# Gate and skip sums all on VectorE, and the token-count product four chunks behind its one-hot rows

## The chip, the cores and the metric

The kernel runs on one core of a Trainium2 chip. The metric is the device time of one execution in microseconds (us); lower is better. The engines named below are TensorE (PE in the profile; PEld is its weight load, which runs beside the products), VectorE (DVE), ScalarE (ACT), GpSimd (POOL) and SyncE (SP), which issues most of the DMAs.

## The reference

Three layers follow one another: attention with head mixing, a dense two-matrix layer, and a mixture of eight experts with a skip. The change lies where the second layer hands over to the third.

```python
def _moe_ref(x, w_in, w_out):                  # 1792 tokens, 768 -> 2048 -> 768
    h = x @ w_in
    g = np.where(h > 0.0, h, np.exp(np.minimum(h, 0.0)) - 1.0)
    return g @ w_out                           # "the second dense product"

def _moe2_ref(x, w_skip, w_gate, w1, w2):      # E = 8 experts, 768 -> 1024 -> 768
    do_compute = x @ w_skip > 0                # the skip sum
    out = x.copy()
    xc = x[do_compute]
    logits = xc @ w_gate                       # the eight gate sums
    e_idx = np.argmax(logits, axis=1)
    ...
    for e in range(E):
        mask = e_idx == e
        h = np.maximum(xc[mask] @ w1[e], 0.0)
        y[mask] = gate_w[mask, None] * (h @ w2[e])
    out[do_compute] = xc + y
    return out
```

## The kernel before, in words

All products are made in a split form: each fp32 operand is a rounded part and a rest, and three products (high by high, low by high, high by low) are summed. The scheduler of the kernel's framework sets the order of instructions on each engine, except in attention, whose order is written by hand. Each engine works through its own list in order, and so does each DMA queue.

**The second dense product** (from 650 us to about 916 us of the span) goes over 14 tiles of 128 tokens, numbered 0 to 13. Each tile sums over 16 chunks of the hidden dimension, n = 0 to 15; a chunk is six products (L859), three for each half of the 768 output columns, so a tile is 96 products. ScalarE and VectorE split the hidden values of the next tile meanwhile (`gh`, L735 and L736, four per tile). When chunk 15 of tile i is done, ScalarE copies the two halves from the accumulators `o` to a row tile `x` (L890), which SyncE writes to DRAM (`x2d` and `out`). The last nine chunks of tile 12 alternate with the first nine of tile 13. In tile 13 the halves have 512 and 256 columns, and from chunk 10 on the wide half is finished first.

**Scoring.** `score` (L740) multiplies the row tile by nine rows of weights (eight gates, one skip, broadcast in `wrow`) and sums each product along the row. Three of the nine products (e = 0, 3, 6) are made on GpSimd (`prod`, L748) and summed on ScalarE (L749); six are multiplied and summed by one VectorE instruction each (`junk`, L755).

**Routing.** `route(i - 1)` is called in tile i behind chunk 11 (15 in tile 1). VectorE finds the best expert (MAX and MAX_INDEX) and makes a one-hot row `oh` per token. TensorE counts tokens per expert in two products into `pp`: ones by `seen` (all tokens before this tile, L778) and an upper triangle by `oh` (L779). VectorE adds `oh` to `seen`, reads the token's place from `pp` (`ps`, `sl`, `slot`, `si`), and GpSimd scatters the token's number and gate weight to its place in `slots` in DRAM (L797).

**The tail.** The first tokens of expert 0 don't go through DRAM for the last two tiles. After `route(11)`, SyncE reads the first 128 places from `slots` into `pre` (L877) and GpSimd gathers their rows from `x2d` into `xp` (L864). For tile 13 the scores are made on TensorE: `score_turned` transposes the row tile (`tx`, L844), ScalarE copies it, and `logits` multiplies it by the gate weights (`lg`, L835). `place_old` (L825) multiplies `xp` by the identity and the rows of tile 12 by a placement matrix `hot` into `pt` (L830, L831); the rows of tile 13 follow (L905). ScalarE and VectorE split `pt` into `xt`, and the first expert's product `ph` (L1056) begins.

Weights of the experts (`w1t`, L1015) are loaded by SyncE as buffers of the second layer come free; the first is split (`whi` on ScalarE, `wlo` on VectorE) during tile 2. After the tail, eight experts follow, to 1101 us.

Of the kernel before, what the change touches and what calls it, by code (L numbers as in the profile page):

```python
# [8 lines left out]
FP32 = mybir.dt.float32  # L9
# [3 lines left out]
ACTF = mybir.ActivationFunctionType  # L13
ALU = mybir.AluOpType
# [5 lines left out]
NT, DM, DFF = B * S, H * D, 2048  # L20
NK = DM // 128
NF = DFF // 128
NTILE = NT // 128
E, F2 = 8, 1024
# [22 lines left out]
OLD = NTILE - 2  # L47
CUT, SPLIT, SKEW = 512, 10, 9
AT_SCORE, AT_ROUTE, AT_FIRST = 8, 18, 11


R0, RC, LOOK = 3, 2, 2
# [382 lines left out]
def mixtures(tc, order, xT, w_in, w_out, w_skip, w_gate, w1, w2, ident, gT, wf, wg, x2d, slots, out):  # L435
# [4 lines left out]
    nc = tc.nc  # L440
    with ExitStack() as top:
# [6 lines left out]
        ones = keep.tile([128, 128], FP32, name="ones")  # L448
        nc.vector.memset(ones, 1.0)
        upper = keep.tile([128, 128], FP32, name="upper")  # L450
# [6 lines left out]
        def behind(op):  # L457
            return tc.issue_after(op.ins) if op else ExitStack()
# [10 lines left out]
        with ExitStack() as ctx:  # L469
# [151 lines left out]
            w = wi[0] = ring_a.tile([128, 2, DM], FP32R, tag="w", name="w")  # L621
# [72 lines left out]
            last = elu(7)  # L694
# [3 lines left out]
            for s in range(2 * B, len(groups)):  # L698
                products(s)
                last = elu(s)  # L700
# [5 lines left out]
        with ExitStack() as ctx:  # L706
# [5 lines left out]
            st_p = pool("st", 3, ctx)  # L712
# [9 lines left out]
            seen = keep.tile([128, E], FP32, name="seen")  # L722
# [17 lines left out]
            def score(x2, cols=slice(0, DM)):  # L740

                lg = st_p.tile([128, E + 1], FP32, tag="lg", name="lg")
                x2, n, part = x2[:, cols], cols.stop - cols.start, 0
                for e in range(E + 1):
                    w = wrow[:, e, cols]
                    if e % 3 == 0:
                        p = st_p.tile([128, DM], FP32, tag="prod", name="prod", bufs=2)
                        nc.gpsimd.tensor_tensor(out=p[:, :n], in0=x2, in1=w, op=ALU.mult)  # L748
                        nc.scalar.activation(out=p[:, :n], in_=p[:, :n], func=ACTF.Copy, accum_out=lg[:, e:e + 1])  # L749
                    else:  # L750
                        if part == 0:
                            t = st_p.tile([128, DM], FP32, tag="junk", name="junk", bufs=1)
                        o = part * n
                        part = (part + 1) % (DM // n)
                        nc.vector.scalar_tensor_tensor(out=t[:, o:o + n], in0=x2, scalar=1.0, in1=w, op0=ALU.mult,  # L755
                                                       op1=ALU.mult, accum_out=lg[:, e:e + 1])
                return lg

            def route(i, lg):
                mx = st_p.tile([128, 8], FP32, tag="mx", name="mx")  # L760
                nc.vector.max(out=mx, in_=lg[:, :E])
                ix = st_p.tile([128, 8], U32, tag="ix", name="ix")
                nc.vector.max_index(out=ix, in_max=mx, in_values=lg[:, :E])
                nmx = st_p.tile([128, 1], FP32, tag="nmx", name="nmx")
                nc.vector.tensor_scalar(out=nmx, in0=mx[:, 0:1], scalar1=-1.0, scalar2=None, op0=ALU.mult)
                ex = st_p.tile([128, E], FP32, tag="ex", name="ex")
                sm = st_p.tile([128, 1], FP32, tag="sm", name="sm")
                nc.scalar.activation(out=ex, in_=lg[:, :E], func=ACTF.Exp, bias=nmx, accum_out=sm)
                nc.vector.tensor_scalar(out=sm, in0=sm, scalar1=1e-9, scalar2=None, op0=ALU.add)
                nc.vector.reciprocal(out=pairs[:, i, 1:2].bitcast(FP32), in_=sm)  # L770
                ef = st_p.tile([128, 1], FP32, tag="ef", name="ef")
                nc.vector.tensor_copy(out=ef, in_=ix[:, 0:1])
                do = st_p.tile([128, 1], FP32, tag="do", name="do")
                nc.vector.tensor_scalar(out=do, in0=lg[:, E:E + 1], scalar1=0.0, scalar2=None, op0=ALU.is_gt)
                oh = st_p.tile([128, E], FP32, tag="oh", name="oh")
                nc.vector.tensor_scalar(out=oh, in0=iota8, scalar1=ef, scalar2=do, op0=ALU.is_equal, op1=ALU.mult)
                pp = ps_r.tile([128, 512], FP32, tag="r", name="pp")
                nc.tensor.matmul(out=pp[:, :E], lhsT=ones, rhs=seen, start=True, stop=False)  # L778
                nc.tensor.matmul(out=pp[:, :E], lhsT=upper, rhs=oh, start=False, stop=True)  # L779
                nc.vector.tensor_tensor(out=seen, in0=seen, in1=oh, op=ALU.add)  # L780
                ps = st_p.tile([128, E], FP32, tag="ps", name="ps")
                sl = st_p.tile([128, 1], FP32, tag="sl", name="sl")
                nc.vector.scalar_tensor_tensor(out=ps, in0=pp[:, :E], scalar=1.0, in1=oh, op0=ALU.mult, op1=ALU.mult,
                                               accum_out=sl)
                big = st_p.tile([128, 1], FP32, tag="big", name="big")
                nc.vector.tensor_scalar(out=big, in0=do, scalar1=-2.0 * E * CAP, scalar2=2.0 * E * CAP, op0=ALU.mult,
                                        op1=ALU.add)
                place = None
                if i >= OLD:
                    place = wg_p.tile([128, 128], FP32, tag=f"hot{i}", name="hot")  # L790
                    nc.vector.tensor_scalar(out=place, in0=iota128, scalar1=sl, scalar2=do, op0=ALU.is_equal,
                                            op1=ALU.mult)
                slot = st_p.tile([128, 1], FP32, tag="slot", name="slot")
                nc.vector.tensor_tensor(out=slot, in0=sl, in1=big, op=ALU.add)
                si = st_p.tile([128, 1], I32, tag="si", name="si")
                nc.vector.tensor_copy(out=si, in_=slot)
                nc.gpsimd.indirect_dma_start(out=slots, out_offset=bass.IndirectOffsetOnAxis(ap=si[:, 0:1], axis=0),  # L797
                                             in_=pairs[:, i, :], in_offset=None, bounds_check=E * CAP - 1,
                                             oob_is_err=False)
                return place  # L800
# [10 lines left out]
            rows = {}  # L811
# [11 lines left out]
            lg = ps_r.tile([128, 512], FP32, tag="r", name="lg")  # L823
# [24 lines left out]
            for i, n, fc, cs in work:  # L848
                last = i == LAST
# [7 lines left out]
                for a, z in THREE:  # L857
                    for c in cs:
                        mm = nc.tensor.matmul(out=po[c][:, :cols[c].stop - cols[c].start],  # L859
                                              lhsT=gs[i][fc // GC][:, a, fc % GC, :], rhs=wo[fc][:, z, cols[c]],  # L860
# [9 lines left out]
                    logits(turned)  # L870
                if last and n == AT_SCORE:
                    scored = score(rows[i - 1])
                if i and n == (15 if i == 1 else AT_ROUTE if last else 11):
                    hot = old_hot = route(i - 1, scored if last else score(rows[i - 1]))
                    if i == OLD:
                        pre = wg_p.tile([128, 2], I32, name="pre")
                        nc.sync.dma_start(out=pre, in_=slots[0:128, :])  # L877
                        xp = wg_p.tile([128, DM], FP32, name="xp")
                        iota128 = wg_p.tile([128, 128], FP32, name="iota128")
                        nc.gpsimd.iota(iota128, pattern=[[1, 128]], base=0, channel_multiplier=0,  # L880
                                       allow_small_or_imprecise_dtypes=True)
                if fc == NF - 1:
                    if 0 in cs:
                        x2 = rows[i] = x2_p.tile([128, DM], FP32, tag="x2", name="x2")
                    for c in cs:
                        to, at = x2[:, cols[c]], po[c][:, :cols[c].stop - cols[c].start]
                        if last and c == 0:
                            nc.vector.tensor_copy(out=to, in_=at)
                        else:
                            nc.scalar.copy(out=to, in_=at)  # L890
                        if last and c == 1:
                            turned, freed = score_turned(x2, c)
                            place_old(range(2))
                            logits(turned)
                            place_old(range(2, 5))
                    if 1 in cs:
                        nc.sync.dma_start(out=x2d[i * 128:(i + 1) * 128, :], in_=x2)
                        if not last:
                            nc.sync.dma_start(out=out[i * 128:(i + 1) * 128, :], in_=x2)
            hot = route(NTILE - 1, lg)  # L900
            place_old(range(5, NK))
            xt0 = [gh_p.tile([128, 2, GC, 128], FP32R, tag="gh", name=f"xt0{c}") for c in range(2)]
            for c in range(2):
                for k in range(3):
                    nc.tensor.matmul(out=pt[c][:, k, :], lhsT=x2[:, (c * 3 + k) * 128:(c * 3 + k + 1) * 128], rhs=hot,  # L905
                                     start=False, stop=(k == 2))
# [410 lines left out]
```

## Time and profile before

| | us |
|---|---|
| median of 3 runs | 1108.67 (1106.9 to 1115.65) |
| profiled execution | 1108.77 |
| its span, first to last instruction | 1107.0 |
| PE busy in the span | 1024.1 (93%) |
| VectorE busy | 802.3 (72%) |
| ScalarE busy | 566.7 (51%) |
| GpSimd busy | 390.7 (35%) |

The span lies 1.77 us under the profiled execution's own time. Rows of the timeline give the start, the length, the engine, the line and operation, what is written from what is read, how many instructions are merged in the row, and in brackets how long the engine idled before and what ended the wait.

### The profile page before, as it was taken

How to read it: one execution, taken by the hardware profiler on the slowest of the kernel's cores; microseconds unless marked ns; L12 is line 12 of the kernel's file. 1: busy time of each engine (PE TensorE's matmuls, PEld its weight loads, DVE VectorE, ACT ScalarE, POOL GpSimd, SP SyncE). 2: the span in 40 equal slices, each digit the busy share in tenths (PEclk: the TensorE clock that was granted, in tenths of full speed). 3: DMA queues.
4: the chain of work that ended last, by engine and by line, in shares of the span. 5: the costliest groups of instructions: out<-in, count | busy, mean ns of one | idle time of the engine just before them, and what ended most of it. 6: DMA issues, size and time to landing. Idle time of an engine off the chain costs nothing. (4 is left out here: it accounts for less than half of the span.)

```text
span 1107.0 us, 29935 instructions
## 1 busy us (share of the span) xinstructions
PE 1024.1 (93%) x12082; PEld 882.8 (80%) x12082; DVE 802.3 (72%) x1495; ACT 566.7 (51%) x1150; POOL 390.7 (35%) x355
## 2 busy tenths in 40 slices
PE   6998999899899888999999999999999989899997
PEld 4676667666677667899999988999999978788887
DVE  5775777677577668667666557878787856999953
ACT  5664656466465555444544454333333326677751
POOL 2232214123221226232232202535354534756521
PEclk8999999999999999999999999999999998999999
DMA  6453564465455556555566557733333385999800
GB/s 202 170 173 109 164 202 138 131 195 182 110 165 173 166 153 225 171 170 157 193 215 206 178 171 262 237 94 107 96 105 107 94 317 184 392 391 343 328 8 32
DMA packets 134218, 199.67 MB, mean 180 GB/s; under 512 B 35860, under 2 KB 101400, under 8 KB 133821
## 3 DMA queue, kind: packets, MB, share of 16 engines
q1 hardware_dynamic: 131933, 191.27, 52.4%
q0 software_dynamic: 2144, 6.46, 1.6%
q8 instruction: 96, 1.57, 0.6%
q14 instruction: 45, 0.37, 0.1%
HBM read 122.47 MB, written 37.65 MB: 145 GB/s over the span
## 5 line engine op out<-in xcount | busy, mean ns | idle before, releaser
L859 PE MATMUL o<-w,gh 128*128 128x384 f32 (+2 forms) x1344 | 242.5, 339 | 2.9 <-ACT w L463 2.4
L585 PE MATMUL h<-xh,w 128*128 128x448 f32 x1152 | 236.3, 367 | 4.7 <-POOL xh L519 4.7
L859 PEld LDWEIGHTS o<-w,gh 128*128 128x128 f32 x1344 | 234.1, 190 | 7.3 <-ACT w L463 3.6
L585 PEld LDWEIGHTS h<-xh,w 128*128 128x128 f32 x1152 | 216.9, 189 | 23.4 <-POOL xh L519 6.5
L236 POOL TENSOR_SCALAR kr<-kpost,rs 128x60 f32<-128x60 f32 x180 | 77.4, 444 | 284.5 <-DVE rs L232 242.7
L252 PEld LDWEIGHTS f<-kr,e 64*64 64x64 f32 (+2 forms) x5760 | 121.2, 138 | 54.6 <-issue 33.5
L755 DVE SCALAR_TENSOR_TENSOR junk<-x,wrow 128x768 f32<-128x768 f32 x78 | 117.1, 1501 | 40.0 <-ACT x L890 38.6
L252 PE MATMUL f<-kr,e 64*64 64x60 f32 (+2 forms) x5760 | 122.4, 225 | 7.3 <-DVE at L258 1.8
L500 POOL TENSOR_TENSOR wf<-a,p 128x768 f32<-128x768 f32 x32 | 66.6, 2082 | 163.3 <-DVE p L498 122.8
L215 DVE TENSOR_REDUCE nmx<-c 128x1 f32<-128x448 f32 x180 | 104.5, 620 | 25.9 <-PE c L206 25.9
L258 ACT COPY at<-f 128x480 f32<-128x480 f32 x96 | 52.5, 547 | 135.2 <-PE f L252 135.2
L1029 DVE TENSOR_TENSOR wlo<-w1t,whi 128x1536 fp32r<-128x1536 f32 x50 | 111.6, 2255 | 13.6 <-ACT whi L1026 13.6
L224 ACT ACTIVATE e<-c,nmx 128x448 f32<-128x448 f32 x180 | 113.0, 637 | 6.3 <-DVE nmx L215 6.3
L1026 ACT CAST whi<-w1t 128x1536 fp32r<-128x1536 f32 x64 | 94.3, 1483 | 34.1 <-PE ph L1056 17.5
L748 POOL TENSOR_TENSOR prod<-x,wrow 128x768 f32<-128x768 f32 x39 | 93.9, 2434 | 50.0 <-ACT x L890 26.8
L154 PE MATMUL qk<-k,qq 64*120 64x448 f32 (+1 forms) x576 | 90.6, 404 | 17.3 <-ACT e L224 10.3
L206 PE MATMUL c<-d,kpre_up 60*64 60x448 f32 x336 | 85.1, 574 | 11.7 <-ACT s L158 11.7
L274 PE MATMUL xp<-at,v 128*64 128x120 f32 (+3 forms) x1536 | 92.2, 267 | 1.4 <-DVE at L258 1.4
L274 PEld LDWEIGHTS xp<-at,v 128*64 128x64 f32 (+1 forms) x1536 | 75.1, 137 | 21.9 <-issue 17.3
L159 DVE TENSOR_SCALAR s<-qk 120x448 f32<-120x448 f32 (+1 forms) x96 | 58.3, 618 | 45.0 <-PE qk L154 19.8
L206 PE MATMUL c<-d,kpre_low 64*64 64x448 f32 x336 | 84.3, 554 | 3.5 <-DMA kpre_low<-kpre_kr 3.5
L154 PEld LDWEIGHTS qk<-k,qq 64*120 64x120 f32 (+1 forms) x576 | 52.8, 180 | 42.1 <-ACT e L224 25.2
(185 smaller groups left out, 1449.2 us busy)
## 6 DMA issues: line engine op xcount, KB each, us to landing
w1t<-in_moe_w_dram SPq DMA_DIRECT2D x64, 768.0 KB
d<-s SPq DMA_DIRECT2D x168, 210.0 KB
gT<-g SPq DMA_DIRECT2D x64, 224.0 KB
f<-in_moe_w_in_dram SPq DMA_DIRECT2D x16, 768.0 KB
f<-in_moe_w_out_dram SPq DMA_DIRECT2D x16, 768.0 KB
gr<-gT SPq DMA_DIRECT2D x48, 256.0 KB
rk<-in_k_dram SPq DMA_DIRECT2D x24, 224.0 KB
xr<-xT SPq DMA_DIRECT2D x24, 224.0 KB
```

The source lines that it names most:

```text
L154: nc.tensor.matmul(out=ps[:n, :S], lhsT=qt[T, p // 2][rows, a, p % 2, :n], rhs=kt[b, p][rows, z, :], start=(i == 0), stop=(i == 2))
L206: nc.tensor.matmul(out=ps[j * UP:(j + 1) * UP, :S], lhsT=kpre_up[UP:UP + HP, :] if z else kpre_low if len(U) == 2 else kpre[:d[z, j].shape ...
L215: nc.vector.tensor_reduce(out=t, in_=c, op=ALU.max, axis=AX.X, negate=True)
L224: nc.scalar.activation(out=e, in_=c, func=ACTF.Exp, bias=t, accum_out=sms[U][:, i:i + 1])
L252: nc.tensor.matmul(out=ps[to, c // 2, :, z, :], lhsT=e[rows, keys], rhs=kr[rows, :])
L274: nc.tensor.matmul(out=ps[z * 64:(z + 1) * 64, i, :n], lhsT=t[:, z, jc % t.shape[2], :], rhs=att[T][:t.shape[0], jc, 2 * p + z, :n], start ...
L585: nc.tensor.matmul(out=ps, lhsT=w[:, a, kk, :], rhs=xs[tb, kk][:, z, :], start=(kk == 0 and a + z == 0), stop=(kk == NK - 1 and a == 1))
L748: nc.gpsimd.tensor_tensor(out=p[:, :n], in0=x2, in1=w, op=ALU.mult)
L755: nc.vector.scalar_tensor_tensor(out=t[:, o:o + n], in0=x2, scalar=1.0, in1=w, op0=ALU.mult, op1=ALU.mult, accum_out=lg[:, e:e + 1])
L859: mm = nc.tensor.matmul(out=po[c][:, :cols[c].stop - cols[c].start], lhsT=gs[i][fc // GC][:, a, fc % GC, :], rhs=wo[fc][:, z, cols[c]], st ...
L1026: nc.scalar.copy(out=hi, in_=t)
L1029: (nc.vector if dve else nc.gpsimd).tensor_tensor(out=lo, in0=t, in1=hi, op=ALU.subtract)
```

## The change

All nine sums of `score` go to VectorE. `route` is cut in two: `route` ends with the one-hot rows, and a new function `seat` begins with the counting products. In tiles 1 to 12 `route(i - 1)` is called behind chunk 11 and `seat` behind chunk 15 (`AT_SEAT`), with its two products held behind the last product issued (`behind(mm)`); in tile 13 both are called at 18, and for tile 13's own tokens one after the other. The read of `pre` follows `seat(11)`. The copy of tile 13's wide half moves from VectorE to ScalarE.

```diff
+AT_SEAT = 15
...
                 for e in range(E + 1):
                     w = wrow[:, e, cols]
-                    if e % 3 == 0:
-                        p = st_p.tile([128, DM], FP32, tag="prod", name="prod", bufs=2)
-                        nc.gpsimd.tensor_tensor(out=p[:, :n], in0=x2, in1=w, op=ALU.mult)
-                        nc.scalar.activation(out=p[:, :n], in_=p[:, :n], func=ACTF.Copy, accum_out=lg[:, e:e + 1])
-                    else:
...
+                    nc.vector.scalar_tensor_tensor(out=t[:, o:o + n], in0=x2, scalar=1.0, in1=w, op0=ALU.mult,
+                                                   op1=ALU.mult, accum_out=lg[:, e:e + 1])
...
                 nc.vector.tensor_scalar(out=oh, in0=iota8, scalar1=ef, scalar2=do, op0=ALU.is_equal, op1=ALU.mult)
+                return i, oh, do
+
+            def seat(i, oh, do, after=None):
+
                 pp = ps_r.tile([128, 512], FP32, tag="r", name="pp")
-                nc.tensor.matmul(out=pp[:, :E], lhsT=ones, rhs=seen, start=True, stop=False)
-                nc.tensor.matmul(out=pp[:, :E], lhsT=upper, rhs=oh, start=False, stop=True)
+                with behind(after):
+                    nc.tensor.matmul(out=pp[:, :E], lhsT=ones, rhs=seen, start=True, stop=False)
+                with behind(after):
+                    nc.tensor.matmul(out=pp[:, :E], lhsT=upper, rhs=oh, start=False, stop=True)
...
-                if i and n == (15 if i == 1 else AT_ROUTE if last else 11):
-                    hot = old_hot = route(i - 1, scored if last else score(rows[i - 1]))
+                if i and n == (AT_ROUTE if last else 11):
+                    routing = route(i - 1, scored if last else score(rows[i - 1]))
+                if i and n == (AT_ROUTE if last else AT_SEAT):
+                    hot = old_hot = seat(*routing, None if last else mm)
...
-                        if last and c == 0:
-                            nc.vector.tensor_copy(out=to, in_=at)
-                        else:
-                            nc.scalar.copy(out=to, in_=at)
+                        nc.scalar.copy(out=to, in_=at)
...
-            hot = route(NTILE - 1, lg)
+            hot = seat(*route(NTILE - 1, lg))
```

**A middle tile, TensorE.** Before, around the counting products of one tile; `o` carries the number of its accumulator:

```order
L859 MATMUL o_11403<-w,gh 128x384
L859 MATMUL o_11404<-w,gh 128x384
L778 MATMUL pp<-seen,ones 128x8
L779 MATMUL pp<-oh,upper 128x8
L859 MATMUL o_11403<-w,gh 128x384
L859 MATMUL o_11404<-w,gh 128x384
```

After, around the same two products:

```order
L861 MATMUL o_11388<-w,gh 128x384
L861 MATMUL o_11389<-w,gh 128x384
L779 MATMUL pp<-seen,ones 128x8
L781 MATMUL pp<-oh,upper 128x8
L861 MATMUL o_11563<-w,gh 128x384
L861 MATMUL o_11564<-w,gh 128x384
```

They stood inside a tile's products, with 24 of the 96 still to come, and now stand between two tiles.

**A middle tile, VectorE.** Before, from the row tile's sums to the one-hot rows and the seats (rows of the search between MAX and `oh` left out):

```order
L755 SCALAR_TENSOR_TENSOR junk,lg<-x_11912,wrow 128x768
L736 TENSOR_TENSOR gh<-gr,gh 128x512
L755 SCALAR_TENSOR_TENSOR junk,lg<-x_11912,wrow 128x768 x3
L736 TENSOR_TENSOR gh<-gr,gh 128x512
L755 SCALAR_TENSOR_TENSOR junk,lg<-x_11912,wrow 128x768 x2
L761 MAX mx<-lg 128x8
```

After, the same stretch:

```order
L751 SCALAR_TENSOR_TENSOR junk,lg<-x_11888,wrow 128x768
L737 TENSOR_TENSOR gh<-gr,gh 128x512
L751 SCALAR_TENSOR_TENSOR junk,lg<-x_11888,wrow 128x768 x3
L737 TENSOR_TENSOR gh<-gr,gh 128x512
L751 SCALAR_TENSOR_TENSOR junk,lg<-x_11888,wrow 128x768 x4
L737 TENSOR_TENSOR gh<-gr,gh 128x512
L751 SCALAR_TENSOR_TENSOR junk,lg<-x_11888,wrow 128x768
L757 MAX mx<-lg 128x8
```

Nine sums instead of six, and three splits of hidden values instead of two, now stand ahead of MAX.

**The tail, TensorE.** Before, from the last products of tile 13 to its placement (this `pp<-oh` is tile 12's; `x_12683` is tile 12's row tile, `x_12744` tile 13's):

```order
L779 MATMUL pp<-oh,upper 128x8
L859 MATMUL o_12526<-w,gh 128x256 x3
L835 MATMUL lg<-wgt,tx 128x9 x4
L859 MATMUL o_12526<-w,gh 128x256 x3
L830 MATMUL pt_10363<-ident,xp 128x128
L831 MATMUL pt_10363<-hot,x_12683 128x128
L830 MATMUL pt_10363<-ident,xp 128x128
L844 MATMUL tx<-ident,x_12744 128x128 x2
L831 MATMUL pt_10363<-hot,x_12683 128x128
```

After, from the same `lg` on (`x_12647` is tile 12's row tile, `x_12705` tile 13's):

```order
L837 MATMUL lg<-wgt,tx 128x9 x4
L861 MATMUL o_12493<-w,gh 128x256 x6
L832 MATMUL pt_10363<-ident,xp 128x128
L832 MATMUL pt_10364<-ident,xp 128x128
L846 MATMUL tx<-ident,x_12705 128x128 x2
L837 MATMUL lg<-wgt,tx 128x9 x2
L781 MATMUL pp<-oh,upper 128x8
L779 MATMUL pp<-seen,ones 128x8
L833 MATMUL pt_10363<-hot,x_12647 128x128
L832 MATMUL pt_10363<-ident,xp 128x128
L833 MATMUL pt_10363<-hot,x_12647 128x128
```

Tile 12's `pp<-oh` moved behind tile 13's logits, and with it all six products of `hot`; eight `pt` products stand between it and tile 13's own `pp<-oh`.

**The tail, SyncE's queue.** Before, around the read of `pre`:

```order
L1015 DMA w1t<-in_moe_w_dram 128x2x768 x4
L877 DMA pre<-slots 128x2
L1015 DMA w1t<-in_moe_w_dram 128x3x512 x2
L897 DMA x2d<-x_12683 128x768
L899 DMA out_dram<-x_12683 128x768
L1015 DMA w1t<-in_moe_w_dram 128x3x512 x3
```

After:

```order
L1016 DMA w1t<-in_moe_w_dram 128x2x768 x4
L1016 DMA w1t<-in_moe_w_dram 128x3x512 x2
L898 DMA x2d<-x_12647 128x768
L900 DMA out_dram<-x_12647 128x768
L881 DMA pre<-slots 128x2
L1016 DMA w1t<-in_moe_w_dram 128x3x512 x3
```

The read of `pre` moved behind two weight loads and the two writes of tile 12's rows, and now stands directly ahead of three weight loads.

## Rows read from the trace of the kernel before

**Rows 1.** Waits of TensorE, 680 to 900 us: total, times, longest.
```profile
PE pp L779 <- DVE oh L776: 8.3, 10, 1.5
PE pp L779 <- issue: 1.2, 1, 1.2
```
**Rows 2.** Timeline of one middle tile, TensorE's weight loads.
```profile
741.20 0.36 PEld L778 LDWEIGHTS pp<-seen,ones 128*128 128x128 f32 x2
...
742.63 16.70 PEld L859 LDWEIGHTS o<-w,gh 128*128 128x128 f32 x96
```
**Rows 3.** Timeline of the same tile, VectorE and GpSimd.
```profile
747.92 7.37 POOL L748 TENSOR_TENSOR prod<-x,wrow 128x768 f32<-128x768 f32 x3 [2.26 <-ACT x L890]
...
748.75 2.33 DVE L736 TENSOR_TENSOR gh<-gr,gh 128x512 fp32r<-128x512 f32 x1
...
751.00 2.60 DVE L755 SCALAR_TENSOR_TENSOR junk<-x,wrow 128x768 f32<-128x768 f32 x1
...
756.15 0.96 DVE L755 SCALAR_TENSOR_TENSOR junk<-x,wrow 128x768 f32<-128x768 f32 x1
...
757.04 0.69 DVE L736 TENSOR_TENSOR gh<-gr,gh 128x512 fp32r<-128x512 f32 x1
...
759.52 0.08 DVE L755 DVE_READ_ACCUMULATOR junk<-x,wrow 128x1 f32 x1
...
760.18 0.29 DVE L776 TENSOR_SCALAR oh<-iota,ef,do 128x8 f32<-128x8 f32 x1
```
**Rows 4.** Timeline at tile 12's counting products.
```profile
890.14 0.36 PEld L778 LDWEIGHTS pp<-seen,ones 128*128 128x128 f32 x2
...
890.64 15.73 PEld L859 LDWEIGHTS o<-w,gh 128*128 128x128 f32 x87
```
**Rows 5.** Timeline of tile 2.
```profile
702.71 0.36 PEld L778 LDWEIGHTS pp<-seen,ones 128*128 128x128 f32 x2
...
704.86 18.25 PEld L859 LDWEIGHTS o<-w,gh 128*128 128x128 f32 x96
...
705.03 1.48 ACT L1026 CAST whi<-w1t 128x1536 fp32r<-128x1536 f32 x1 [0.41 <-DMA w1t<-in_moe_w_dram]
...
706.54 1.76 DVE L1029 TENSOR_TENSOR wlo<-w1t,whi 128x1536 fp32r<-128x1536 f32 x1 [1.09 <-ACT whi L1026]
```
**Rows 6.** Busy time (PE, PEld, DVE, ACT, POOL), granted clock, DMA share, GB/s.
```profile
707.00:709.00 2.00, 2.00 (x8) 2.00 (x7) 2.00 (x6) 0.02 (x1) 0.00 (x0) 0.50 1.05 326
```
**Rows 7.** Timeline, from tile 11's scatter to the gather of `xp`.
```profile
891.69 1.01 POOL L797 DMA_INDIRECT slots<-pairs,si x1 [9.76 <-DVE si L796]
897.41 0.34 SPq L877 DMA_DIRECT2D pre<-slots  x1
...
899.39 1.05 POOL L864 DMA_INDIRECT xp<-x2d,pre x1 [6.69 <-DMA pre<-slots]
```
**Rows 8.** DMA issues, 897 to 911 us: issues, us from issue to landing.
```profile
xp<-x2d,pre POOLq DMA_INDIRECT x1, 7.4
```
**Rows 9.** The scatters of all 14 tiles, landing.
```profile
DMA to landing us min/median/max: 2.1/3.6/6.7
```
**Rows 10.** Timeline of the tail, TensorE and VectorE.
```profile
910.49 0.68 DVE L888 COPY x<-o 128x512 f32<-128x512 f32 x1
...
911.32 1.09 PE L844 MATMUL tx<-ident,x 128*128 128x128 f32 x4 [4.61 <-DVE load L930]
...
918.18 0.55 PEld L830 LDWEIGHTS pt<-ident,xp 128*128 128x128 f32 x2
...
918.60 0.55 PEld L831 LDWEIGHTS pt<-hot,x 128*128 128x128 f32 x2
...
920.14 0.18 DVE L761 MAX8 mx<-lg 128x8 f32<-128x8 f32 x1 [6.02 <-PE lg L835]
...
922.90 1.41 PEld L905 LDWEIGHTS pt<-hot,x 128*128 128x128 f32 x12 [0.74 <-DVE hot L791]
...
924.41 1.66 PE L1056 MATMUL ph<-whi,xt 128*128 128x512 f32 x6
```

More of the change, by code (lines that the diff above doesn't have):

```diff
@@ L745, in score @@
                     w = wrow[:, e, cols]
-                    if e % 3 == 0:
-                        p = st_p.tile([128, DM], FP32, tag="prod", name="prod", bufs=2)
-                        nc.gpsimd.tensor_tensor(out=p[:, :n], in0=x2, in1=w, op=ALU.mult)
-                        nc.scalar.activation(out=p[:, :n], in_=p[:, :n], func=ACTF.Copy, accum_out=lg[:, e:e + 1])
-                    else:
[L751 to L756, printed above, removed]
+                    if part == 0:
+                        t = st_p.tile([128, DM], FP32, tag="junk", name="junk", bufs=1)
+                    o = part * n
+                    part = (part + 1) % (DM // n)
+                    nc.vector.scalar_tensor_tensor(out=t[:, o:o + n], in0=x2, scalar=1.0, in1=w, op0=ALU.mult,
+                                                   op1=ALU.mult, accum_out=lg[:, e:e + 1])
                 return lg
```

## The prediction

> **What bounds the kernel now.** I read the waits of TensorE first. While the second dense product runs, TensorE waits for one thing alone, the one-hot rows that its counting product needs: 8.3 us in ten waits, and 1.2 us in tile 1, which the profile puts down to "issue" [rows 1]. The timeline of one tile shows the size: from the first counting load to the next ordinary one pass 1.43 us (741.20 to 742.63), and the tile's 96 loads take 16.70 us, so a tile lasts 18.13 us [rows 2]. Tile 12, whose one-hot rows were early, shows the same two products without a wait: 0.50 us (890.14 to 890.64) [rows 4]. The difference, 0.93 us, is what a wait costs a middle tile.
>
> Why the rows are late is in VectorE's part of that tile. While GpSimd makes its three products (747.92 to 755.29), a sum on VectorE takes 2.60 us and a split 2.33; as soon as GpSimd is done, the same shapes take 0.96 and 0.69 [rows 3]. So GpSimd's help is paid for by VectorE, which stands still while GpSimd reads.
>
> The tail has a second stall: TensorE idles 4.61 us ahead of the transposes of tile 13's wide half, because VectorE copies that half (910.49) only behind tile 12's scores [rows 10].
>
> **The change, part by part.**
>
> *Nine sums on VectorE.* A sum is 0.96 us and its accumulator read 0.08, 1.04 at most when they don't overlap [rows 3]; nine are 9.4 us. Four splits at 0.69 are 2.8. The search and `oh` took 0.95 us (759.52 to 760.47) [rows 3], and the seat's small instructions I put at as much again, an estimate from that row. VectorE thus needs about 14.1 us of a tile that will last 16.70 + 0.50 = 17.2. It doesn't become the bound. GpSimd's and ScalarE's removed work was on no path but this one, so taking it away gives nothing by itself.
>
> *Counting four chunks later.* The sums start when the row tile is copied, some 1.1 us into a tile (742.63 plus 24 loads of 0.174 us makes 746.8; GpSimd starts at 747.92 [rows 2, 3]). Then 9.4 of sums, three splits (2.1) and 0.95 put `oh` at 13.5 us of the tile; the counting product now comes at 16.7. It is covered by 3.2 us. Nothing that TensorE needs hangs on the seats in the middle tiles: the scatter ends in DRAM, and `seen` is wanted a tile later. So tiles 3 to 11, nine of the ten waits, give 9 x 0.93 = **8.4 us**.
>
> *Tile 2.* Its wait was 2.15 us between loads (702.71 to 704.86), 1.65 above the unhindered 0.50, and its 96 loads took 18.25 instead of 16.70 [rows 2, 5], because the granted clock was down to 0.50, the lower level of 1.2 GHz, behind that wait [rows 6]. Together 3.2 us. But in the new order the weight split `wlo` (1.76 us) stands ahead of `oh`, and it waits for `whi`, which waits for a weight load [rows 5]. By the old times `wlo` would end at 708.3 (706.54 and 1.76), while TensorE asks at about 706 (702.71 plus 24 loads of 0.174, less the 0.9 us won in tile 1, below); the load may come earlier, since the splits that free SyncE's queue do. Bounds: all 3.2, or a loss of 1.0 where the wait grows. I take half a microsecond of wait and no drop of the clock: **2.7 us**.
>
> *Tile 1.* The wait of 1.2 us [rows 1] lies behind the tile, and `pp<-oh` is moved 13 products on. The one-hot rows now follow a sum of the next row tile, so I take 0.3 off: **0.9 us**, bounds 0 and 1.2.
>
> *The copy of the wide half, to ScalarE.* ScalarE has nothing else then, since its three summing passes are gone, and the products that stand behind the copy hide it. The 4.61 us of idling go. What is late next is `xp`.
>
> *The read of `pre`, moved with the seat.* From the point where tile 12's chunk 11 ends (890.14), 48 products of 0.174 us and the counting come first, so the scatter starts not at 891.69 but at 891.69 + 8.35, about 900.05 in the old time scale. Scatter to read was 5.7 us, read to gather 2.0 [rows 7]; with a scatter of median landing, 3.6 [rows 9], the gather starts at 905.7 to 906, instead of 899.39, and lands 7.4 us later [rows 8], at **913.4**. The read now holds up three weight loads in SyncE's queue until the scatter has landed. They belong to experts that come later, so nobody waits for them soon, but they then run beside the gather, as loads did before. TensorE gets to `xp` much sooner: counting at 898.5 to 899.0, then 60 less 48 products (2.1), 18 wide ones and 18 narrow ones (0.235 and 0.118 us each, since the 87 loads in 15.73 us [rows 4] are 60 of 384 columns, 18 of 512 and 9 of 256: 4.2 + 2.1), and nine small pairs at 0.235 (six pairs in 1.41 us [rows 10]: 2.1), which ends at **909.5**. It waits 3.9 us for `xp`.
>
> *The rest of the tail.* Behind the old stall the clock was at the lower level; pairs of `pt` products followed one another every 0.42 us (918.18 to 918.60), while the later ones took 0.235 [rows 10]. I expect the same behind the new one. From 913.4: six pairs at 0.42 and ScalarE's copy of the transposes, 3.0 us, so tile 13's logits end at 916.4, where before they ended at 920.14. But `hot` of tile 12 is now made behind MAX of tile 13 and wants `pp<-oh` first, about 1.3 us; then eight `pt` pairs (3.4 us) stand ahead of tile 13's own `pp<-oh` (0.42), another 1.0 us to its `hot`, and 1.5 from there to the first `ph` (922.90 to 924.41 [rows 10]). The sum is 924.0, against 924.41: **0.4 us**. Nearly all that the lost stall gives is taken by the wait for `xp` and by products that used to run beside VectorE's search.
>
> The bounds are far apart. With `xp` in time and the clock up, the logits end at 911.5, `ph` starts at 917: 7.4 us. With the gather 2 us later, the tail loses 1.6.
>
> The Trainium skill ("DMA: Bandwidth & Descriptors", section "SWDGE vs HWDGE vs iDMA") says that DMAs issued by GpSimd and those issued by SyncE sit in different queues of an engine, which takes them in turn. By that the gather would not stand behind the weight loads, and the first rival below would be the likelier one; the landing of 7.4 us for 128 rows of 3 KB [rows 8] speaks against a large share for it.
>
> **The sum.** 8.4 + 2.7 + 0.9 + 0.4 = 12.4 us. The profiled execution took 1108.77 us, span 1107.0; it stands 0.1 us above the median of 1108.67, so the two need no correction. The experts behind the tail are shifted as a whole: their loads wait for buffers, not for the clock on the wall. Forecast: 1108.7 - 12.4 = **1096.3 us**, 1.1% faster.
>
> **The rivals.**
>
> *The gather is in time.* If scatter, read and gather land in 9.5 us together, TensorE doesn't wait for `xp`, and the clock may stay up. For it: the shortest scatter lands in 2.1 us [rows 9], and the rule above. Against it: one gather of 7.4. It gives 7.0 us more: 1089.3.
>
> *New waits take more.* Tile 2 waits for `wlo` as long as it did for `oh`, and the clock drops there again (nothing won, perhaps 1.0 lost), and `xp` lands 2 us later. Then 8.4 + 0.9 - 1.0 - 1.6 = 6.7, so 1102.0. For it: the order of `wlo`, and the scatter's longest landing of 6.7.
>
> *VectorE becomes the bound; slower.* If GpSimd is not what stretches VectorE, but something that stays (the copies, the DMAs), four sums at 2.6, five at 1.04 and a split at 2.33 make 15.6 + 4.4 + 1.9 = 21.9 us a tile, above the old 18.1: 11 tiles x 3.8 = 42 us slower, 1150. It decides from a mean of 1.34 us a sum on ((18.1 - 4.1 - 1.9) / 9). Against it: both shapes fall back to their short time the moment GpSimd ends [rows 3].
>
> *The gap closes at one place and opens at the next*, the one-hot rows still late at the new place: gain only tail, 1106 or so. It needs 3.2 us more than I count on VectorE.
>
> **How the numbers follow.** Forecast 0.50 (1093.5 to 1099); gather in time 0.20; more waits 0.22; slower 0.04; no gain 0.04. The range of 8 in 10 leaves out the last two and a part of the second and third: 1089.5 to 1102. A change within 1% (1097.6 to 1119.8) is about what a measurement can't tell from none. Faster by more: the second case and four fifths of the first, 0.60; slower by more 0.04; the rest 0.36.
>
> **What would show it.** TensorE's waits for `oh` gone from the middle tiles, which repeat every 17.2 us; every sum near 0.96 us; in tile 2 the gap ahead of `pp<-oh` shows which bound held; in the tail a wait of 2 to 5 us ahead of the first product with `xp`, with the gather issued 6 to 7 us after the scatter, and the granted clock at 0.50 behind it. I am wrong if sums stay long without GpSimd, if `xp` is no wait, or if the experts' stage itself changes its length.

## The result, and the profile after

| | before | after |
|---|---|---|
| median, 17 runs each, us | 1111.74 | 1101.89 |
| lowest to highest, us | 1106.9 to 1122.17 | 1098.75 to 1108.37 |
| span of the profiled execution, us | 1107.0 | 1104.1 |
| VectorE / ScalarE / GpSimd busy, us | 802.3 / 566.7 / 390.7 | 776.6 / 533.5 / 301.0 |

The ratio is 0.9914, with a 95% interval of 0.989 to 0.9938: some 9.6 us of the 12.4 that were forecast, at a time that is 5.6 us above the forecast one. The kernel before, run 14 times more, has a median 3.1 us above that of the three runs which the forecast started from; the rest, 2.5 us, is the change's own.

The two spans differ by 2.9 us only, and hide what the change did: the layers ahead of it, whose code is the same, brought this execution to the first counting product 7.9 us later (PE's `pp<-seen` at 696.48, against 688.56). So I compare a stretch that begins with the change: from the first `pp<-seen`, which stands behind chunk 15 of tile 1 in both kernels, to the first `ph`. It is 235.85 us before (to 924.41) and 225.25 after (to 921.73): **10.6 us**. From `ph` to the end pass 182.59 and 182.37, so the experts' stage has not changed.

The waits of TensorE in the stretch of the change, 640 to 925 us: total, times, longest.

```profile
PE pt L832 <- DMA xp<-x2d,pre: 6.3, 1, 6.3
PE o L861 <- ACT w L464: 1.9, 2, 1.7
...
PE pp L779 <- DVE ps L785: 0.3, 1, 0.3
```

The waits for `oh`, 8.3 us and 1.2 [rows 1], are gone from all tiles, the second one too; a counting product waits once, 0.3 us in the tail, and the 1.9 us are for weights of the dense layer itself. What has come is one wait of 6.3 us for `xp`.

One middle tile, timeline of VectorE and of TensorE's loads (start, length, engine, operation):

```profile
742.32 0.17 DVE L757 MAX8 mx<-lg 128x8 f32<-128x8 f32 x1
...
742.98 0.29 DVE L772 TENSOR_SCALAR oh<-iota,ef,do 128x8 f32<-128x8 f32 x1
...
747.82 0.36 PEld L779 LDWEIGHTS pp<-seen,ones 128*128 128x128 f32 x2
748.10 0.30 PEld L781 LDWEIGHTS pp<-oh,upper 128*128 128x128 f32 x2
748.33 11.84 PEld L861 LDWEIGHTS o<-w,gh 128*128 128x128 f32 x68
```

The one-hot rows are ready at 743.27, TensorE asks at 747.82: 4.5 us of cover, and 0.51 us from the counting loads to the next ordinary one, where a waiting tile showed 1.43 [rows 2]. The reason is in the view of two tiles, the sums and the splits (least, median and greatest duration in ns):

```profile
L751 DVE SCALAR_TENSOR_TENSOR junk<-x,wrow x117: 947/957/1006, 686.3 to 902.8; 128x768 f32<-128x768 f32 x117
...
L737 DVE TENSOR_TENSOR gh<-gr,gh x56: 673/690/695, 659.4 to 878.3; 128x512 fp32r<-128x512 f32 x56
```

No sum is stretched any more, and no split; before, single ones took 2.60 and 2.33 us [rows 3].

The tail, timeline of the engines that hand on the first tokens of expert 0:

```profile
895.18 1.43 POOL L799 DMA_INDIRECT slots<-pairs,si  x1 [24.12 <-DVE si L798]
...
900.55 0.33 SPq L881 DMA_DIRECT2D pre<-slots  x1
...
900.97 1.45 SPq L1016 DMA_DIRECT2D w1t<-in_moe_w_dram  x3
...
903.24 1.46 POOL L866 DMA_INDIRECT xp<-x2d,pre  x1 [6.62 <-DMA pre<-slots]
...
910.90 1.22 PE L832 MATMUL pt<-ident,xp 128*128 128x128 f32 x4 [6.35 <-DMA xp<-x2d,pre]
...
921.73 1.66 PE L1057 MATMUL ph<-whi,xt 128*128 128x512 f32 x6
```

The read of `pre` follows the scatter by 5.37 us, the gather follows the read by 2.69, and TensorE can use `xp` 7.66 us after the gather's start: 15.72 us from scatter to `xp`, of which TensorE stands for the last 6.35. Busy time, granted clock (third number from the end), DMA share and GB/s in the same stretch:

```profile
894.00:896.00 2.00, 2.00 (x13) 1.77 (x13) 1.71 (x8) 0.69 (x2) 0.82 (x1) 1.00 1.04 404
896.00:898.00 2.00, 2.00 (x12) 1.65 (x11) 1.93 (x5) 0.00 (x0) 0.61 (x1) 1.00 0.92 355
898.00:900.00 2.00, 2.00 (x10) 1.67 (x9) 1.93 (x5) 0.00 (x0) 0.00 (x0) 1.00 0.08 29
...
908.00:910.00 2.00, 0.00 (x0) 0.00 (x0) 0.00 (x0) 0.00 (x0) 0.00 (x0) 0.50 1.00 304
910.00:912.00 2.00, 1.09 (x5) 1.10 (x6) 0.00 (x0) 0.00 (x0) 0.00 (x0) 0.50 1.01 406
```

Two things are to be seen: the scatter starts while the DMA engines are full, with the last of seven weight loads and the two row writes of tile 12, and they are full again, with the next loads and tile 13's row writes, while TensorE waits for the gather; and the granted clock goes to 0.50, the lower level of 1.2 GHz, while TensorE stands.

### The profile page after: what moved, and what is told of

The parts are those of the page before. It is cut to its first block, busy times and chain, and to the rows that moved or that the text cites. A ratio compares the mean times of both kernels' runs of the same rounds, so it can differ in the third digit from the quotient of the medians.

```text
span 1104.1 us, 29895 instructions
## 1 busy us (share of the span) xinstructions
PE 1028.6 (93%) x12082; PEld 881.5 (80%) x12082; DVE 776.6 (70%) x1572; ACT 533.5 (48%) x1073; POOL 301.0 (27%) x316
## 5 line engine op out<-in xcount | busy, mean ns | idle before, releaser
L586 PE MATMUL h<-xh,w 128*128 128x448 f32 x1152 | 240.9, 370 | 4.5 <-POOL xh L520 4.4
L861 PE MATMUL o<-w,gh 128*128 128x384 f32 (+2 forms) x1344 | 239.6, 337 | 2.3 <-ACT w L464 1.9
L861 PEld LDWEIGHTS o<-w,gh 128*128 128x128 f32 x1344 | 231.5, 188 | 6.3 <-ACT w L464 2.8
L751 DVE SCALAR_TENSOR_TENSOR junk<-x,wrow 128x768 f32<-128x768 f32 x117 | 111.8, 955 | 3.4 <-ACT x L891 1.0
L1027 ACT CAST whi<-w1t 128x1536 fp32r<-128x1536 f32 x64 | 94.3, 1482 | 35.8 <-PE ph L1057 17.2
L155 PE MATMUL qk<-k,qq 64*120 64x448 f32 (+1 forms) x576 | 90.1, 401 | 17.7 <-ACT e L225 10.7
L275 PE MATMUL xp<-at,v 128*64 128x120 f32 (+3 forms) x1536 | 94.5, 271 | 1.4 <-DVE at L259 1.4
L736 ACT CAST gh<-gr 128x512 fp32r<-128x512 f32 x56 | 35.0, 624 | 100.7 <-PE o L861 41.6
```

The source lines that it names most:

```text
L155: nc.tensor.matmul(out=ps[:n, :S], lhsT=qt[T, p // 2][rows, a, p % 2, :n], rhs=kt[b, p][rows, z, :], start=(i == 0), stop=(i == 2))
L275: nc.tensor.matmul(out=ps[z * 64:(z + 1) * 64, i, :n], lhsT=t[:, z, jc % t.shape[2], :], rhs=att[T][:t.shape[0], jc, 2 * p + z, :n], start ...
L586: nc.tensor.matmul(out=ps, lhsT=w[:, a, kk, :], rhs=xs[tb, kk][:, z, :], start=(kk == 0 and a + z == 0), stop=(kk == NK - 1 and a == 1))
L1027: nc.scalar.copy(out=hi, in_=t)
```

## The experiments

Two theories. **A**: the change's loss is one seat, the count of tile 11's tokens, which starts the way to `xp`; put four chunks later, it ends 8 us later, and all other tiles would not need to be late at all. **B**: the sums on VectorE or ScalarE's copy cost something in the tail. Then, within A: why that way takes 15.7 us where I counted 13.3.

All results, with the stretch from the first `pp<-seen` to the first `ph` in the profiled execution (in the two kernels with the seat at 11, `pp<-seen` comes 24 products sooner, so 24 x 0.174 = 4.2 us are taken off):

| kernel | median, us | ratio to before, 95% interval | stretch, us | gain in it | `ph` to end |
|---|---|---|---|---|---|
| the change | 1101.89 | 0.9914 [0.989, 0.9938] | 225.25 | 10.6 | 182.37 |
| tile 11's count early | 1094.08 | 0.9828 [0.9798, 0.9858] | 215.37 | 20.5 | 182.86 |
| sums only, seat at 11 | 1094.16 | 0.984 [0.9814, 0.9865] | 216.8 | 19.1 | 182.77 |
| seat only, old sums | 1098.81 | 0.9881 [0.9858, 0.9905] | 223.95 | 11.9 | 182.59 |
| copy back on VectorE | 1103.92 | 0.9925 [0.9896, 0.9954] | 224.91 | 10.9 | 182.29 |
| sums only, `hot` first | 1093.18 | 0.9822 [0.9786, 0.9858] | 215.2 | 20.7 | 182.71 |
| row writes behind `pre` | 1101.39 | 0.9904 [0.9871, 0.9937] | 225.56 | 10.3 | 182.24 |
| three loads held | 1100.25 | 0.9892 [0.9845, 0.9939] | 219.58 | 16.3 | 184.48 |
| ten loads held | 1105.26 | 0.9931 [0.9905, 0.9957] | 218.84 | 17.0 | 193.53 |

The gain in the stretch, less what the experts' stage loses, orders the kernels as the measured ratios do, but for neighbours whose intervals overlap; so the readings below rest on traces that stand for the times.

**1. Tile 11's count early, the others late.**

```diff
-                if i and n == (AT_ROUTE if last else AT_SEAT):
+                if i and n == (AT_ROUTE if last else 11 if i == OLD else AT_SEAT):
```

> The change, but in tile 12 alone the counting products come behind chunk 11 again, so the scatter of tile 11, the read of pre and the gather of xp start 8.3 us sooner. Theory A (the tail waits for the gather): TensorE's wait of 6.3 us ahead of the first product with xp is gone; the time is 6 to 9 us under that of the change (9 if the clock also stays up), about 1094. Theory B (the tail is long because tile 12's products of hot stand behind tile 13's logits, and the wait only overlaps that): the wait goes and turns up again as waits for hot and pp; within 2 us of the change, about 1101.

Timeline of the tail:

```profile
886.53 0.97 POOL L799 DMA_INDIRECT slots<-pairs,si  x1 [15.77 <-DMA w1t<-in_moe_w_dram]
894.04 1.05 POOL L866 DMA_INDIRECT xp<-x2d,pre  x1 [6.54 <-DMA pre<-slots]
...
904.12 0.60 PE L832 MATMUL pt<-ident,xp 128*128 128x128 f32 x4
...
911.54 0.73 PE L1057 MATMUL ph<-whi,xt 128*128 128x512 f32 x2
```

The gather starts 10.08 us ahead of the first product with `xp`, which finds it there: no wait, the clock stays at 1.00, and `ph` follows 7.42 us behind, where the change needed 10.83. The time is below the change's by 7.8 us as the medians stand, and by 0.86% of the time before as the ratios do. Theory A holds: one seat of twelve cost all of it.

**2. The sums alone, the seat back at 11.**

```diff
-AT_SEAT = 15
+AT_SEAT = 11
```

> Nine sums on VectorE, and the counting products behind chunk 11 in all tiles: the deferral undone, the sums kept. Theory A (the one-hot rows were late because GpSimd held VectorE up): in the middle tiles the rows are ready at 12.2 us of the tile and TensorE asks at 12.5, so hardly any wait comes back (under 0.3 us a tile), and xp is in time as well; 1 us either side of the first experiment, about 1094 to 1096. Theory B (the deferral is what removes the waits): 0.6 to 0.9 us in each of ten tiles comes back, 6 to 9 us above the first experiment, about 1102.

TensorE waits for `oh` only once here, for 0.2 us, and not for `xp` (gather at 887.53, first product at 897.36). The time is that of the first experiment. So the deferral, half of the change, brings nothing beside the sums on VectorE, and costs 8 us.

**3. The seat alone, with GpSimd's three products.**

The old body of `score` (three of nine products on GpSimd and ScalarE) in the changed kernel.

> The counting products behind chunk 15, three of nine sums on GpSimd as before: the sums undone, the deferral kept (the wide half's copy stays on ScalarE). Theory A: the waits in the middle tiles are gone here too, since the rows came 1 us late and now have 4; in the tail the scheduler puts tile 12's pp and hot ahead of tile 13's logits again, so that behind the gather only some 8.4 us are left instead of 10.8: 2.5 us under the change, about 1099, with a wait for xp as in the change. Rival (VectorE held up by GpSimd still delays something TensorE needs, splits above all): waits for gh or for oh in the tiles, 5 us or more above the change, 1107.

Waits of TensorE, 640 to 925 us:

```profile
PE tx L851 <- ACT x L896: 3.7, 1, 3.7
...
PE pp L786 <- issue: 1.2, 1, 1.2
```

The median came as expected, though its interval overlaps the change's; the way to it came only in part. From the first product with `xp` to `ph` pass 8.16 us, where 8.4 were expected. The waits for `oh` are gone but for tile 1's 1.2 us, so either remedy alone cures them, and the two do not add. But the tail has no wait for `xp`: TensorE stands ahead of `tx` instead, because ScalarE's copy of the wide half stands behind its summing passes, and these wait for GpSimd. The clock falls behind that wait as it fell before the change; TensorE reaches `xp` only at 905.45, with a gather that started at 898.20.

The same kernel shows most plainly what GpSimd does to VectorE. Timeline of a middle tile:

```profile
744.99 6.65 DVE L756 SCALAR_TENSOR_TENSOR junk<-x,wrow 128x768 f32<-128x768 f32 x1
...
745.37 5.45 POOL L749 TENSOR_TENSOR prod<-x,wrow 128x768 f32<-128x768 f32 x3
```

One sum on VectorE lasts from 0.38 us before GpSimd's three products to 0.82 us behind them: 6.65 us, where the next takes 0.96.

**4. The wide half's copy back on VectorE.**

```diff
-                        nc.scalar.copy(out=to, in_=at)
+                        if last and c == 0:
+                            nc.vector.tensor_copy(out=to, in_=at)
+                        else:
+                            nc.scalar.copy(out=to, in_=at)
```

> The change with the copy of tile 13's wide half back on VectorE. Theory A (the old stall is only hidden behind the wait for xp): TensorE idles some 3 us ahead of the transposes and that much less ahead of xp; the time is that of the change within 1 us, about 1102. Rival (the stall and the wait add up): 3 us above the change, 1105.

The only long wait is again that for `xp`; the 3 us ahead of the transposes, which the first theory expected beside it, are not there:

```profile
PE pt L832 <- DMA xp<-x2d,pre: 6.0, 1, 6.0
```

The time can't be told from the change's: the two intervals overlap. With the sums on VectorE, the stall of 4.61 us [rows 10] doesn't come back with the copy; the scheduler puts three products more ahead of `tx` (39 instead of 36). With experiment 2, which keeps the sums and is fast, Theory B has nothing left to stand on.

**5. The sums alone, with `hot` ahead of the last logits.** The second experiment, and the last tile's logits behind tile 12's `pp<-oh`:

```diff
-                            logits(turned)
+                            logits(turned, counted[0])
```

> The sums on VectorE with the counting product back at seat 11, and the logits of the last tile ordered behind tile 12's `pp<-oh`, so that VectorE forms `hot` of tile 13 right behind the maximum. Theory A (the change's own loss is the late pair of `xp`, and what is left in the tail is the order between the last logits and the products of the counts): from `lg` to `ph` in about 4.5 us instead of the 5 to 7 of the two kernels with an early scatter, 0.5 to 1.5 us under the kernel with the sums alone, that is 1092.5 to 1094 by its median of 1094.2. Rival: `pp<-oh` itself waits for `oh` and holds the logits up by more than a microsecond; same time or up to 1096.

```profile
902.81 0.29 PE L781 MATMUL pp<-oh,upper 128*128 128x8 f32 x2
...
908.89 1.67 PE L1059 MATMUL ph<-whi,xt 128*128 128x512 f32 x6
```

From the first `lg` of the narrow half (903.43) to `ph` pass 5.46 us, not the 4.5 that the first theory expected, against 7.15 in experiment 2 (898.88 to 906.03), where the clock was down, and 5.89 in experiment 1 (905.65 to 911.54). It has the lowest median of all kernels here, 1093.18, but its interval overlaps those of experiments 1 and 2: by measurement the three can't be told apart.

**6. Why is the way to `xp` long? The row writes behind `pre`.** In the change, SyncE issues tile 12's two row writes beside the scatter; here they come behind the read.

```diff
+                        with behind(pre_in if i == OLD else None):
+                            nc.sync.dma_start(out=x2d[i * 128:(i + 1) * 128, :], in_=x2)
```

(and the same for `out`.)

> The change, with tile 12's two row writes (`x2d`, `out`) issued behind the read of `pre`. Theory A1 (the two writes that are issued with the scatter share its time, and stretch the way from the scatter to the start of the gather to 8.1 us): this way takes about 5.9 us, the wait of `pt<-xp` falls from 6.3 to about 4, and the time from 1102 to about 1100. Rival A2 (the way is the scatter's own, its landing and the read of `pre` each taking what they take in a quiet queue): 7.5 us or more, and the same time as the change within 1 us.

```profile
893.11 1.44 POOL L799 DMA_INDIRECT slots<-pairs,si  x1 [24.11 <-DVE si L798]
...
898.68 0.34 SPq L881 DMA_DIRECT2D pre<-slots  x1
...
901.26 1.36 POOL L866 DMA_INDIRECT xp<-x2d,pre  x1 [6.72 <-issue]
```

5.57 and 2.58 us, together 8.15, where the change had 8.06. The forecast of A1 fails, and the time is the change's. But the edit moved more than the row writes. SyncE's weight loads ahead of the scatter, in the change and here:

```profile
878.30 12.91 SPq L1016 DMA_DIRECT2D w1t<-in_moe_w_dram  x7
```

```profile
876.23 15.01 SPq L1018 DMA_DIRECT2D w1t<-in_moe_w_dram  x8
```

An eighth weight load of 768 KB has moved up into the place of the two row writes of 384 KB, and the writes now lie beside the gather, with 7.0 us of waiting for `xp`. So as many bytes stand ahead of the scatter as in the change, and this run alone does not clear the row writes. Two others do: the kernel before has weight loads but no row writes there, and takes 5.72 us from scatter to read [rows 7]; experiment 8 below has the row writes without the loads, and takes 3.08. That one also speaks against the reason that A2 gives, a way of the scatter's own.

**7. Three weight loads held.** The three that SyncE issues right behind the read wait for tile 13's row write.

```diff
-                    with behind(wrow_in if len(raws) < R0 else None):
+                    with behind(wrow_in if len(raws) < R0 else row_out if 10 <= len(raws) < 13 else None):
```

> The change, with the three weight loads that are issued behind the read of `pre` held until tile 13's row write. Theory B1 (the loads run beside the gather and share its DMA engines, so that it lands in 7.7 us): the gather lands in 4.5 to 6 us, the wait of `pt<-xp` falls by 2 to 3 us, the time to about 1099.5, unless the first expert then waits for its weights. Rival B2 (the landing is the gather's own, row by row): 7 us or more again, the time as the change's within 1 us, or later by what the weights are late.

```profile
891.34 1.43 POOL L799 DMA_INDIRECT slots<-pairs,si  x1 [24.12 <-DVE si L798]
...
896.02 0.33 SPq L881 DMA_DIRECT2D pre<-slots  x1
...
898.70 1.16 POOL L866 DMA_INDIRECT xp<-x2d,pre  x1 [5.92 <-DMA pre<-slots]
...
902.48 0.71 PE L832 MATMUL pt<-ident,xp 128*128 128x128 f32 x4 [1.76 <-DMA xp<-x2d,pre]
```

`xp` is there 3.78 us after the gather's start, half of the 7.66 of the change and less than the 4.5 to 6 that were expected. B1 holds: the loads beside the gather took the other half. The tail gains 5.7 us in the stretch, 3.9 of them here, but the first experts lose part of it again, in a wait that the change has at 1.2 us:

```profile
PE ph L1057 <- DVE xt L1047: 6.2, 1, 6.2
```

The last instructions of VectorE and GpSimd ahead of it:

```profile
936.20 4.17 POOL L1030 TENSOR_TENSOR wlo<-w1t,whi 128x1536 fp32r<-128x1536 f32 x1
...
937.02 3.37 DVE L965 COPY cum<-cum 1x8 f32<-1x8 f32 x1
```

VectorE's split `xt` stood behind a copy of eight numbers that took 3.37 us, beside a weight split on GpSimd, where the same copy took 0.15 at 933.54. So the wait is VectorE's; that the held loads brought it about is not shown. The stage from `ph` on is 2.1 us longer. The median is 1.6 below the change's, and the intervals overlap; the trace shows the mechanism, the times do not settle its worth.

**8. Ten weight loads held.** The seven that are issued ahead of the scatter (878 to 891 us in the change) are held as well: `3 <= len(raws) < 13` in the line above.

> As the run before (three loads held until tile 13's row write), and the seven weight loads that are issued ahead of the scatter held there too, so that neither the scatter nor the read of `pre` has weight loads in front of it. Theory C1 (the way from scatter to gather is long because the scatter's rows lie behind the loads that were issued in the 17 us before it): scatter to the issue of `pre` in 3.5 to 4 us, the median of the quiet tiles, against 4.7 to 5.6 in the kernels with the loads; the gather lands in 3.7 us again; `xp` then is there about when TensorE comes, with a wait of 1 us or none. Rival C2 (the loads have nothing to do with the scatter; the landing takes this long when `pre` reads behind it): 4.7 us or more again. In time this kernel should lose: ten loads of 768 KB come late, so the first experts wait for their weights, and I expect 1103 to 1115.

```profile
889.03 1.43 POOL L799 DMA_INDIRECT slots<-pairs,si  x1 [24.12 <-DVE si L798]
...
892.11 0.33 SPq L881 DMA_DIRECT2D pre<-slots  x1
...
894.73 1.81 POOL L866 DMA_INDIRECT xp<-x2d,pre  x1 [4.26 <-DMA pre<-slots]
...
899.40 0.71 PE L832 MATMUL pt<-ident,xp 128*128 128x128 f32 x4 [0.99 <-DMA xp<-x2d,pre]
```

Scatter to read is 3.08 us now, below the 3.5 to 4 that were expected; read to gather stays at 2.62; `xp` lands after 4.67, about a microsecond more than expected, of which 0.65 us is GpSimd's own issue of the gather (1.81 us long, 1.16 in experiment 7). The whole way is 10.37 us instead of 15.72. C1 holds: loads that were issued up to 17 us earlier made the scatter late. The scatter's packets show where: the first moves 2.5 us behind its start in the change, in experiment 7 and here, the last 4.75, 4.06 and 2.68 us behind it. In time the kernel loses that again, as expected, at the first experts (`ph` to the end is 11.2 us longer); the waits there are for splits of the hidden values, and that late weights stand behind them is argued, not shown:

```profile
PE y L1070 <- DVE ht L1047: 6.6, 1, 6.6
PE y L1070 <- ACT ht L1046: 6.5, 1, 6.5
```

## Why the prediction was wrong, by its own steps

**The middle tiles: right.** Nine tiles, tile 2 and tile 1 were forecast at 12.0 us together. From the first `pp<-seen` to the end of tile 12's chunk 11 the trace shows 201.75 us before (688.39 to 890.14, loads) and 188.97 after (696.31 to 893.63 less 48 x 0.174): 12.8. Tiles repeat every 17.18 us (17.2 forecast). The 0.8 more is mostly tile 2, where I took 2.7 of the 3.2 us for fear of `wlo`: there was no wait, and the clock stayed at 1.00 from 700 to 720 us.

**VectorE: right, with more cover than counted.** A sum takes 0.96 and a split 0.69; `oh` ends 4.5 us ahead of its product, 3.2 forecast. That GpSimd was the cause, and not the copies or the DMAs, is shown by experiment 2, which takes GpSimd's products away and leaves the seat and those other suspects of the middle tiles where they were, and by the sum of 6.65 us in experiment 3. The Trainium skill ("SBUF — State Buffer", section "Who interferes with whom") says that a VectorE instruction with two inputs in SBUF contends with a GpSimd instruction that reads there; the traces agree, at 6.65 us against 0.96.

**The tail: the step that failed.** The prediction wrote "with a scatter of median landing, 3.6 [rows 9], the gather starts at 905.7 to 906", which put the way from scatter to gather at 5.9 us. It was 8.06. The scatter started where it was forecast (895.18 is 900.04 in the old time scale, shifted by 4.86 so that tile 12's chunk 11 ends together; forecast 900.05), TensorE reached `xp` at 909.4 (909.5), the gather took 7.66 (7.4), and `ph` followed `xp` by 10.83 (10.6). So the wait was 6.35 instead of 3.9, and the tail lost 2.2 us (34.27 to 36.45) where 0.4 were to be won. Most scatters behind the median ran in tiles whose only DMAs are row writes and hidden values; this one had the weight loads ahead of it, as the scatter of [rows 7] had, which stands next to it in the trace and took 5.7 + 2.0 = 7.70. With that row the sum would have been: gather at 907.75, `xp` at 915.15, `ph` at 925.75, a tail of -1.3 and 10.7 us in all, against the 10.6 of the trace. That the two agree so closely is luck: the middle tiles gave 0.8 more than forecast, and the tail 0.9 less than by that row. The price came from many rows in other conditions where one row in the same condition stood by. Of the 2.2 us that the way was too long, the scatter has some 1.5 to 1.8 and the read the rest: from read to gather pass 2.69 us, not 2.0, and they stay at 2.62 without a weight load in front (experiment 8). What makes that link longer in the kernels with the late seat stays open.

Experiments 7 and 8 show what these conditions are: of 15.72 us from scatter to `xp`, 1.6 to 2.3 are loads ahead of the scatter (5.37 in the change and 4.68 in experiment 7, to 3.08) and 3.0 to 3.9 loads beside the gather (7.66 to 4.67 or 3.78). The prediction used the 7.4 us of [rows 8] rightly, but as the gather's own price. The Trainium skill ("DMA: Bandwidth & Descriptors", section "SWDGE vs HWDGE vs iDMA") has the DMA engines take their queues in turn. The packets do not show it here. The DMA queues of the change behind the gather's start, 903.24 to 907.9 us (packets, MB, share of the 16 engines; q1 is SyncE's queue, q0 GpSimd's):

```profile
q1 hardware_dynamic: 918, 1.81, 101.7%
```

and of experiment 7, 898.7 to 902.2 us:

```profile
q0 software_dynamic: 80, 0.35, 32.6%
q1 hardware_dynamic: 17, 0.05, 3.8%
```

In the change no packet of the gather moves for 4.7 us, while SyncE's queue moves 1.81 MB; at its first packet, 907.98, some 2.0 of the 2.36 MB of the three loads issued ahead of it are through. With these loads held, all its 80 packets are through within 3.5 us. So the gather did stand behind most of the loads issued ahead of it, and the rule gave no ground for the first rival, in which the gather comes in time. The kernel before has the same sign: from the gather's start, 899.39, to its first packet at 903.70 SyncE's queue moves 1.45 MB.

**The rivals.** Half of the second came true: `xp` 2.4 us later than forecast (910.90 is 915.76 in the old scale, 913.4 forecast), tile 2 not. That its time, 1102.0, is nearly the measured 1101.89 is luck: it gave a gain of 6.7 us, some 9.6 were measured, and the higher base made up for it. For the same reason the measured time lies above the forecast's own 1093.5 to 1099 and only 0.1 us inside the range of 8 in 10. The first rival's bound for a tail without the wait, 7.4 us, is what experiment 1 shows: 20.5 in the stretch less 12.8 makes 7.7. VectorE as the bound, and a gap that moves on, did not come.

**The base.** The forecast started from the median of three runs, which lay 3.1 us under that of 17, more than the 2.5 us by which the gain was mis-sized. Of the 5.6 us between the forecast time and the measured one, the greater half is this.

## What to carry to other kernels

Deferring a product defers everything that hangs on its result: cost the longest chain behind it (here scatter, read, gather, 15.7 us), not only the engine that no longer waits, and let the one tile that feeds the chain keep its early place. Price a DMA by the row that shares its neighbours in the queues, not by the median of the quiet ones. And take a change of two remedies for one wait apart: either cured it here, and the one that was not needed cost 8 us.

## What the runs showed of the hardware that I had not expected

- A VectorE sum of 0.96 us lasted 6.65 us beside three GpSimd products in a row, though it began 0.38 us before them; in the kernel before, the same two kinds of instruction took turns at 2.60 and some 2.46 us each (7.37 us for three) [rows 3]. GpSimd had its three done in 5.45 us.
- A scatter of 128 small rows was finished, by the read that waits for it, 3.08 us after its start with two row writes ahead of it, and 4.6 to 5.8 us in the nine kernels with weight loads ahead; a gather of 128 rows of 3 KB landed after 3.7 and 4.6 us without weight loads in front, and after 6.9 to 8.2 us in the eight kernels with them, in the change with its first packet only 4.74 us behind its start.
- The granted clock does not answer the same idling in the same way each time. Experiments 1 and 2 have the same pattern of small gaps behind the last logits (TensorE busy for 0.98, 0.54, 0.73 and 0.93 us of four microseconds, then full). In experiment 2 the clock then fell, in experiment 1 it didn't:

```profile
901.00:902.00 1.00, 1.00 (x9) 1.00 (x8) 0.77 (x6) 0.00 (x0) 0.94 (x1) 0.71 1.06 408
902.00:903.00 1.00, 1.00 (x7) 1.00 (x7) 0.00 (x0) 0.00 (x0) 0.00 (x0) 0.50 1.03 412
```

and of experiment 1, at the same place behind the gaps:

```profile
908.00:909.00 1.00, 1.00 (x12) 1.00 (x11) 0.54 (x4) 0.00 (x0) 0.71 (x1) 1.00 1.03 409
```

What sets this apart stays open.
